# Hash products and sums of the late attention pairs grouped ahead of a half's scores, and weight stores on GpSimd's queue: one change to an attention and SwiGLU kernel

## Chip, cores and metric

The kernel runs on one core of a Trainium2 chip. The metric is the device time of one execution in microseconds (us), the median of several. The engines are TensorE (PE: matmuls; PEld are its weight loads), VectorE (DVE), ScalarE (ACT), GpSimd (POOL) and SyncE (SP); POOL, SP and ACT can issue DMA transfers, each from a queue of its own that is worked in order.

## What is computed

Attention in which a query sees only the keys of its own hash bucket (the signs of six projections), over 4 batches and 8 heads of 768 positions by 64, and behind it a SwiGLU block on the 3072 x 512 result.

```python
q_bits = (einsum('bhsd,dk->bhsk', q, proj) > 0)          # 6 bits, same for k
mask = q_bucket[:, :, :, None] == k_bucket[:, :, None, :]
scores = where(mask, scale * (q @ k.T), -1e9)
attn = exp(scores - max) / (sum + 1e-9)
x = (attn @ v).transpose(0, 2, 1, 3).reshape(3072, 512)
g = x @ w_gate;  val = x @ w_val
out = (g * sigmoid(g) * val) @ w_out                     # d_ff 1536
```

The three weight matrices arrive as 8-byte floats, of which the kernel makes single-precision parts itself.

## The kernel before

**Attention.** Two heads make a pair; 16 pairs are worked one after the other (n from 0 to 15), each in two halves of 384 query rows (half 0 and 1). A half has six key chunks of 128. For each chunk `score` (L436 to L450) runs the score products and on top of them the hash products of q and k signs (`qb`, `kb`), so that keys of another bucket drop out, and ACT writes the exponentials into one of eight buffers `A`. DVE adds the exponentials up in `acc` (`add`, L478 and L482). Behind the six chunks, `attend` (L460) multiplies them by v, and ACT copies the result to `xT` (L471).

The score, hash, sum and transpose products take their PSUM tiles from one pool, "ps", of 7 banks in rotation: an eighth tile waits until the first one's last reader is through.

For each pair there is work besides:

- the operands of the next pair (`front`). For late pairs (n + 1 > 4) two DVE transposes (L413) come behind half 0's scores, and then one group of eight hash products (L372) whose tile ACT reads in four sign operations (L377). `hash_next` does the two q signs at once, sends them to a second place by a DMA on SP (L389), and returns the two k signs and DVE's mask products (L386) as a list `rest` for later. Before, the group stands behind chunk 2 of half 1, and `rest` is worked behind all six chunks.
- the sums of the pair before (`total`, L487 to L499): four products of `acc` with ones (L493), a copy on ACT (`row`, L496), a DMA to `few` (L498). Then `invert` (L502 to L511): a reciprocal on DVE, a DMA to DRAM (`sums`) and two back (`r`); then `norm` (L517) multiplies on DVE and stores `xT` (L522). Before, the sums stand behind chunk 1 of half 0, `invert` behind half 0's scores, and `norm` behind half 1's.
- loads of the pair after next on SP: q and k (L271, eight DMAs behind chunk 2 of half 1, in runs of 128 bytes for late pairs) and v (L250).
- four or five steps of the weight preparation (`prepare`), which fill idle time of DVE and ACT.

**Weight preparation.** 36 pieces. For each one, POOL loads `words` (L120), ACT scales them (`scale`, L127 and L128) into a `stage` buffer (three of them), DVE does three steps (L153, L155, L158), ACT rounds (`round_up`, L135), DVE does two more (L167, L169), and a DMA stores the buffer to DRAM (`ram`, L171). `scale_ahead` (L137) scales the next piece i if i < kept + ahead, where kept is the number of pieces whose store has been issued; ahead is 3 in attention and is set to 2 ahead of the gated block. Scaling piece i overwrites the buffer of piece i-3, so it waits until that store has landed. 26 stores are issued by the end of attention, on POOL; for the other ten, and the last seven `words` loads, `queues[0]` is SP.

**The gated block.** Per batch 12 blocks of hidden columns: for each one ("U"), a gate piece g and a value piece v, each with products "a" and "n" of 2.8 and 1.4 us on PE (L600), ACT's copy of a (L642), DVE's subtraction (L648), SiLU (L650), the product (L652) and the hidden parts (L653 to L658); after each three, the output products ("D", six chunks). Their PSUM tiles are four, of two banks each, in rotation ("pp"). Weight pieces come from DRAM through a ring of seven buffers (`bring`, L207, on POOL). Behind each of these atoms (four in a U, six in a D) the loop calls `prepare_on(1)` and then `scale_ahead()`, so one step of the weight preparation follows each atom.

The order on each engine is that of the program text, and waits between engines are set by the framework from the data.

Of the kernel before, what the change touches and what calls it, by code (L numbers as in the profile page):

```python
# [8 lines left out]
FP32 = mybir.dt.float32  # L9
# [10 lines left out]
def kernel(  # L20
# [20 lines left out]
    nc = tc.nc  # L41
# [8 lines left out]
    NP = H // 2  # L50
# [27 lines left out]
    def r32(t):  # L78
        return t.bitcast(FP32R)

    def finish(todo):
        while todo:
            todo.pop(0)()
# [12 lines left out]
    n = 0  # L96
# [8 lines left out]
    NPIECE = len(pieces)  # L105
    ram = [dram.tile([P, 3, PIECE], FP32R, tag=f"ram{i}", name="ram") for i in range(NPIECE)]
    words = {}
    staged = {}
    progress = {"scaled": 0, "kept": 0, "ahead": 3}

    queues = [nc.gpsimd]

    def load_words(count, queue=None):
        queue = queue or queues[0]
        for i in range(len(words), min(count, NPIECE)):
            words[i] = t = wordp.tile([P, PIECE, 2], I32, tag="words", name="words")
            to = t.rearrange("p f w -> p (f w)")
            if len(pieces[i].shape) == 3:
                to = to.rearrange("p (j c) -> p j c", j=NJ)
            queue.dma_start(to, pieces[i])  # L120

    def scale(i):
        t = words[i]
        staged[i] = st = stagep.tile([P, 3, PIECE], FP32, tag="stage", name="stage")
        top = t.rearrange("p f w -> p (f w)").bitcast(U16)
        top = top.rearrange("p (f w) -> p f w", w=4)[:, :, 1]
        nc.scalar.activation(st[:, 1], t[:, :, 1].bitcast(FP32), AF.Copy, scale=2.0**-112)  # L127
        nc.scalar.activation(t[:, :, 0], top, AF.Copy, scale=2.0**-13 * (1 + 2.0**-17))  # L128
        progress["scaled"] = i + 1
# [3 lines left out]
    def round_up():  # L133
        st = staged[unrounded.pop(0)]
        nc.scalar.activation(r32(st[:, 0]), st[:, 1], AF.Copy, scale=TOWARD)  # L135

    def scale_ahead():  # L137
        if unrounded:
            round_up()
        i = progress["scaled"]  # L140
        if i < NPIECE and i < progress["kept"] + progress["ahead"] and i in words:
            scale(i)

    def prepare():
        for i in range(NPIECE + 1):
            if i < NPIECE:
                load_words(i + 1)
                if i not in staged:
                    scale(i)
                t, st = words[i], staged[i]  # L150
                lo, hi = t[:, :, 0], t[:, :, 1]
                wi = st[:, 1].bitcast(I32)
                nc.vector.tensor_single_scalar(wi, wi, 3, op=ALU.logical_shift_left)  # L153
                yield True
                nc.vector.scalar_tensor_tensor(out=wi, in0=hi, scalar=-(1 << 31), in1=wi,  # L155
                                               op0=ALU.bitwise_and, op1=ALU.bitwise_or)
                yield True
                nc.vector.tensor_tensor(wi, wi, lo, op=ALU.add)  # L158
                unrounded.append(i)
                load_words(i + 3)  # L160
                yield True
            if i > 0:
                while i - 1 in unrounded:
                    round_up()
                st = staged[i - 1]
                w = st[:, 1]
                nc.vector.tensor_tensor(r32(w), w, st[:, 0], op=ALU.subtract)  # L167
                yield True
                nc.vector.scalar_tensor_tensor(out=r32(st[:, 2]), in0=w, scalar=-STEP,  # L169
                                               in1=st[:, 0], op0=ALU.mult, op1=ALU.add)  # L170
                queues[0].dma_start(ram[i - 1].bitcast(FP32), st)  # L171
                progress["kept"] = i
                yield True

    preparing = prepare()

    def prepare_on(n):
        for _ in range(n):
            next(preparing, None)
# [51 lines left out]
    def attention(scope):  # L231
# [44 lines left out]
        def load(n, names):  # L276
            if n < len(pairs):
                for name in names:
                    fetch(n, name, nc.sync)
# [151 lines left out]
        waiting = []  # L431
# [4 lines left out]
        def score(u):  # L436
            n, half, c = units[u]
            qs = slice(half * HQ, (half + 1) * HQ)
            ks = slice(c * P, (c + 1) * P)
            sc = [bank("sc")[:, 0:HQ] for _ in range(2)]  # L440
            for x, start in ((T, True), (bits, False)):
                if u < 2 and not start:
                    prepare_pair(1)
                for h in range(2):
                    rows = slice(h * D, (h + 1) * D)
                    nc.tensor.matmul(sc[h], x["k", n][rows, ks], x["q", n][rows, qs],  # L446
                                     start=start, stop=not start)
            for h in range(2):
                nc.scalar.activation(weights(u)[:, h, 0:HQ], sc[h], AF.Exp,  # L449
                                     scale=SCALE * (OFF / 2 if n <= NP else 1.0))  # L450
# [22 lines left out]
        def add(u):  # L473
            n, half, c = units[u]
            a = weights(u)
            if c == 1:
                acc[n, half] = att.tile([P, 2, HQ], FP32, tag="acc", name="acc", bufs=3)
                nc.vector.scalar_tensor_tensor(out=acc[n, half], in0=weights(u - 1)[:, :, 0:HQ],  # L478
                                               scalar=S * EPS / P, in1=a[:, :, 0:HQ],
                                               op0=ALU.add, op1=ALU.add)  # L480
            elif c > 1:
                nc.vector.tensor_tensor(acc[n, half], acc[n, half], a[:, :, 0:HQ], op=ALU.add)  # L482
# [4 lines left out]
        def total(n):  # L487
            ps = bank("sum")
            t = [acc.pop((n, half)) for half in range(2)]
            for h in range(2):  # L490
                for half in range(2):
                    g = (2 * h + half) * BLOCK
                    nc.tensor.matmul(ps[g : g + BLOCK, 0:HQ], ones, t[half][:, h, :],  # L493
                                     start=True, stop=True)
            row = att.tile([P, HQ], FP32, tag="row", name="row", bufs=1)
            nc.scalar.copy(row, ps[:, 0:HQ])  # L496
            few = small.tile([P, each], FP32, tag="few", name="few")
            nc.sync.dma_start(few, row.rearrange("(g r) t -> r g t", r=BLOCK)[0])  # L498
            waiting.append(lambda: invert(n, few))  # L499
# [27 lines left out]
        rest = []  # L527

        def prepare_pair(count):
            for _ in range(count):  # L530
                if steps:
                    rest.extend(f for f in steps.pop(0)() or [] if f)
# [4 lines left out]
        last = []  # L537
        for u in range(0, N, NCH):
            n, half, _ = units[u]
            more = n + 1 < len(pairs)  # L540
            for c in range(NCH):
                score(u + c)
                if u + c == 2 or more and half == 1 and c == 2:
                    prepare_pair(1)
                if half == 1 and c == 2:
                    load(n + 2, "qk")
                if c == 1 and half == 0 and n > 0:
                    total(n - 1)
                if c:
                    add(u + c)  # L550
            finish(rest)
            if half == 0 and more:
                steps = front(n + 1)
                if u:
                    prepare_pair(2)
            if half == 0:
                while waiting:
                    last.append(waiting.pop(0)())
            else:
                finish(last)  # L560
            for _ in range(1 if u else 2):
                scale_ahead()
            for c in range(NCH):
                attend(u + c)
            scale_ahead()
            if half == 1:
                load(n + 2, "v")
            elif more:
                if n + 1 <= NP:
                    prepare_pair(2 if u else 4)  # L570
            prepare_on(5 if 0 < n < NP else 4)
            if u >= N - 7 * NCH:
                bring()
# [5 lines left out]
    with ExitStack() as scope:  # L579
        attention(scope)  # L580
# [3 lines left out]
    def gated_block(scope):  # L584
        rest = scope.enter_context(tc.tile_pool(name="odd_x_rest", bufs=1))
# [118 lines left out]
                        end(c)  # L704
                    yield chunk

        queues[0] = nc.sync
        progress["ahead"] = 2
        tails = []
        splits = []  # L710
        count = [0]
# [27 lines left out]
    with ExitStack() as scope:  # L739
        gated_block(scope)  # L740
# [32 lines left out]
```

## Time and profile before

| | |
|---|---|
| median of 3 runs | 961.79 us (961.63 to 964.93) |
| the profiled execution's own time | 961.79 us |
| its span | 960.0 us |
| attention, about | 0 to 358.6 us |
| gated block, about | 358.6 us to the end |
| one late pair where nothing waits | 20.12 us (hash group to hash group, 259.42 to 279.54) |
| a `ring` load, 768 KB | 5.6 us from issue to landing (median) |
| a `ram` store on POOL, 768 KB | 4.7 us (median of 26) |

The span runs from the first to the last instruction. In a row of the timeline, the first two numbers are start and length in us; then come engine, line, operation and operands, how many instructions were merged, and in brackets the idle time ahead of the row and what ended it. A line number is one of the kernel before; the changed kernel's numbers differ by up to 7.

### The profile page before, as it was taken

The numbers are of one execution on the slowest core, as the hardware profiler recorded it, in microseconds if no ns is written. First come the engines' busy times: TensorE is split into PE (matmuls) and PEld (weight loads), VectorE is DVE, ScalarE is ACT, GpSimd is POOL, SyncE is SP. The second block draws the span as 40 slices with busy tenths as digits, with TensorE's granted clock in tenths as the row PEclk, the third lists the DMA queues.
The fourth block names the chain that finished last, engine by engine and source line by source line (L and its number), as shares of the span: only waits on it lengthen the run. The fifth ranks groups of instructions, "written<-read, shape, count | busy, mean of one in ns | idle before, by whom it ended". The sixth has DMA issues, their size and how long they took to land.

```text
span 960.0 us, 14459 instructions
## 1 busy us (share of the span) xinstructions
PE 938.3 (98%) x5413; PEld 715.0 (74%) x5413; DVE 672.0 (70%) x868; ACT 473.7 (49%) x882; POOL 114.7 (12%) x231
## 2 busy tenths in 40 slices
PE   8999989999999799999999999999999999999997
PEld 4444434444444349999999999999999999999996
DVE  4788878888888586878766545766546686446556
ACT  6899777777877565443331332421332422332311
POOL 3110011100101011111111011011111111110100
PEclk9999999999999899999999999999999999999999
DMA  6567567886888868896676565565754655754641
GB/s 187 161 179 205 141 168 200 193 214 173 228 191 251 204 227 295 304 386 262 255 263 250 194 232 191 186 218 207 282 197 141 238 204 184 270 196 134 237 158 67
DMA packets 135798, 203.22 MB, mean 212 GB/s; under 512 B 92912, under 2 KB 100560, under 8 KB 135728
## 3 DMA queue, kind: packets, MB, share of 16 engines
q0 software_dynamic: 28560, 148.26, 43.5%
q1 hardware_dynamic: 106368, 53.84, 21.4%
q8 instruction: 43, 0.70, 0.3%
q10 hardware_dynamic: 800, 0.20, 0.1%
q14 instruction: 27, 0.22, 0.1%
HBM read 162.01 MB, written 39.42 MB: 210 GB/s over the span
## 4 chain that ended last, share of the span: by engine, by line
PE 89%; DMA 4%; ACT 2%; SPq 2%; DVE 2%; issue 1%; ACTq 0%; DVEq 0%; POOLq 0%
PE a L600 28%; PE o L600 20%; PE sc L446 14%; PE n L600 14%; PE av L460 10%; DMA qb<-qb 3%; SPq L271 2%; ACT A L449 1%; PE sum L493 1%; PE hps L372 1%; PE tps L359 1%; DMA xram<-xT 1%; ACT qb L377 1%; DVE o L692 0%; DVE o L689 0%
## 5 line engine op out<-in xcount | busy, mean ns | idle before, releaser
L600 PE MATMUL a<-xparts,ring 128*128 128x384 f32 x1536 | 282.2, 334 | 0.6 <-ACT row L496 0.6
L600 PEld LDWEIGHTS a<-xparts,ring 128*128 128x128 f32 x1536 | 268.1, 188 | 2.5 <-ACT row L496 1.3
L600 PE MATMUL o<-ring,hid 128*128 128x512 f32 x864 | 199.1, 390 | 0.0
L600 PEld LDWEIGHTS o<-ring,hid 128*128 128x128 f32 x864 | 161.9, 188 | 33.1
L449 ACT ACTIVATE A<-sc 128x384 f32<-128x384 f32 x384 | 157.7, 508 | 21.7 <-PE sc L446 21.2
L446 PE MATMUL sc<-qT,kT 64*128 64x384 f32 x768 | 165.6, 505 | 0.2 <-ACT A L449 0.2
L600 PE MATMUL n<-xparts,ring 128*128 128x384 f32 x768 | 148.5, 334 | 0.0
L482 DVE TENSOR_TENSOR acc<-acc,A 128x768 f32<-128x768 f32 x128 | 122.7, 958 | 23.5 <-ACT A L449 12.2
L207 POOL DMA_DIRECT2D ring<-ram x144 | 75.9, 529 | 494.8 <-PE n L600 321.6
L600 PEld LDWEIGHTS n<-xparts,ring 128*128 128x128 f32 x768 | 134.5, 188 | 0.0
L460 PE MATMUL av<-A,vraw 128*64 128x386 f32 (+1 forms) x768 | 131.2, 490 | 0.0
L648 DVE TENSOR_TENSOR v<-v,n 128x768 f32<-128x768 f32 x48 | 45.8, 954 | 111.4 <-PE n L600 109.6
L446 PEld LDWEIGHTS sc<-qT,kT 64*128 64x128 f32 x768 | 69.4, 189 | 70.9 <-issue 53.0
L460 PEld LDWEIGHTS av<-A,vraw 128*64 128x64 f32 x768 | 52.3, 136 | 71.9 <-issue 59.1
L642 ACT ACTIVATE g<-a 128x768 f32<-128x768 f32 x48 | 39.0, 812 | 126.3 <-PE a L600 126.3
L653 ACT ACTIVATE hid<-v 128x768 fp32r<-128x768 f32 x48 | 40.7, 848 | 119.9 <-DVE v L652 119.9
L650 ACT ACTIVATE g<-g 128x768 f32<-128x768 f32 x48 | 40.6, 846 | 87.6 <-DVE g L648 87.6
L692 DVE TENSOR_TENSOR o<-o 128x512 f32<-128x512 f32 x96 | 66.0, 687 | 21.5 <-ACT o L687 19.0
L446 PE MATMUL sc<-qb,kb 64*128 64x384 bf16 x384 | 68.8, 325 | 6.2 <-DMA qb<-qb 4.4
L648 DVE TENSOR_TENSOR g<-g,n 128x768 f32<-128x768 f32 x48 | 45.6, 950 | 34.2 <-PE n L600 31.0
L656 DVE SCALAR_TENSOR_TENSOR hid<-hid,v 128x768 fp32r<-128x768 f32 x48 | 45.9, 957 | 26.9 <-ACT hid L653 26.9
L689 DVE SCALAR_TENSOR_TENSOR o<-o 128x512 f32<-128x512 f32 x72 | 49.5, 687 | 12.0 <-PE o L600 11.4
(77 smaller groups left out, 671.1 us busy)
## 6 DMA issues: line engine op xcount, KB each, us to landing
ring<-ram POOLq DMA_DIRECT2D x144, 768.0 KB, 5.6
ram<-stage POOLq DMA_DIRECT2D x26, 768.0 KB, 4.7
ram<-stage SPq DMA_DIRECT2D x10, 768.0 KB
vraw<-in_v_dram SPq DMA_DIRECT2D x16, 384.0 KB
out_dram<-o SPq DMA_DIRECT2D x24, 256.0 KB
r<-sums SPq DMA_DIRECT2D x30, 192.0 KB
qraw<-in_q_dram SPq DMA_DIRECT2D x48, 96.0 KB
words<-in_moe_w_gate_dram POOLq DMA_DIRECT2D x9, 512.0 KB, 7.0
```

The lines of the kernel that those rows point to most:

```text
L207: nc.gpsimd.dma_start(t.bitcast(FP32), ram[at].bitcast(FP32))
L446: nc.tensor.matmul(sc[h], x["k", n][rows, ks], x["q", n][rows, qs], start=start, stop=not start)
L449: nc.scalar.activation(weights(u)[:, h, 0:HQ], sc[h], AF.Exp, scale=SCALE * (OFF / 2 if n <= NP else 1.0))
L460: nc.tensor.matmul(ps[h * D : (h + 1) * D, 0:width], raws["v", n][:, h, c, :], a[:, h, 0:width], start=c == 0, stop=c == NCH - 1)
L482: nc.vector.tensor_tensor(acc[n, half], acc[n, half], a[:, :, 0:HQ], op=ALU.add)
L600: nc.tensor.matmul(ps, w, x, start=start, stop=stop)
L648: nc.vector.tensor_tensor(two(z), two(z), n_, op=ALU.subtract)
L650: nc.scalar.activation(z, z, AF.Silu)
L653: nc.scalar.activation(h, val, AF.Copy, scale=TOWARD / STEP)
L656: nc.vector.scalar_tensor_tensor(out=l, in0=h.bitcast(FP32), scalar=-STEP, in1=val, op0=ALU.mult, op1=ALU.add)
L689: nc.vector.scalar_tensor_tensor(out=accs[c], in0=t[:, 0], scalar=STEP + 1, in1=accs[c], op0=ALU.mult, op1=ALU.add)
L692: nc.vector.tensor_tensor(accs[c], accs[c], t[:, 1], op=ALU.subtract)
```

## The change

In attention:

- `total(n - 1)` moves from behind chunk 1 of half 0 to ahead of half 1's scores (pairs 1 to 14; the last pair keeps its place).
- For late pairs the hash group moves from behind chunk 2 of half 1 to ahead of half 1's scores, right behind the sums. Its k signs and DVE's mask products follow behind chunk 1 of that half instead of behind its last chunk.
- `invert` moves behind half 1's scores, and `norm` behind the next pair's half 0.

In the weight preparation, the switch of queue and of `ahead` is gone: stores and words stay on POOL, and `ahead` stays 3 in the gated block.

```diff
-    progress = {"scaled": 0, "kept": 0, "ahead": 3}
-    queues = [nc.gpsimd]
-    def load_words(count, queue=None):
-        queue = queue or queues[0]
+    progress = {"scaled": 0, "kept": 0}
+    def load_words(count, queue=nc.gpsimd):
...
-        if i < NPIECE and i < progress["kept"] + progress["ahead"] and i in words:
+        if i < NPIECE and i < progress["kept"] + 3 and i in words:
             scale(i)
...
-                queues[0].dma_start(ram[i - 1].bitcast(FP32), st)
+                nc.gpsimd.dma_start(ram[i - 1].bitcast(FP32), st)
...
             more = n + 1 < len(pairs)
+            final = not more
+            late = n + 1 > NP
+            if half == 1 and n > 0 and not final:
+                total(n - 1)
+            if half == 1 and more and late:
+                prepare_pair(1)
             for c in range(NCH):
                 score(u + c)
-                if u + c == 2 or more and half == 1 and c == 2:
+                if u + c == 2 or more and half == 1 and c == 2 and not late:
                     prepare_pair(1)
+                if half == 1 and c == 1 and late:
+                    finish(rest)
                 if half == 1 and c == 2:
                     load(n + 2, "qk")
-                if c == 1 and half == 0 and n > 0:
+                if c == 1 and half == 0 and final:
                     total(n - 1)
...
+            if half == 1:
+                finish(last)
+            while waiting and (half == 1 or final):
+                last.append(waiting.pop(0)())
             if half == 0:
-                while waiting:
-                    last.append(waiting.pop(0)())
-            else:
-                finish(last)
+                finish(last[:-1] if final else last)
+                last[:] = last[-1:] if final else []
...
-        queues[0] = nc.sync
-        progress["ahead"] = 2
```

## The prediction

> **What bounds it now.** I read the page's busy shares and chain first, then busy time by stage, then the order of events on each engine around the moved instructions. The chain of what ended last is TensorE (PE) nearly everywhere:
>
> ```profile
> PE 938.3 (98%) x5413; PEld 715.0 (74%) x5413; DVE 672.0 (70%) x868; ACT 473.7 (49%) x882; POOL 114.7 (12%) x231
> ...
> PE 89%; DMA 4%; ACT 2%; SPq 2%; DVE 2%; issue 1%; ACTq 0%; DVEq 0%; POOLq 0%
> ```
>
> So each term below is a change of PE's time: an instruction group that gets shorter, or a gap. By stage (columns: window, its length, then busy us of PE, PEld, DVE, ACT, POOL, clock, DMA share, GB/s):
>
> ```profile
> 110.00:358.60 248.60, 234.46 (x1550) 102.23 (x1546) 205.48 (x277) 184.62 (x419) 24.95 (x42) 0.98 0.76 201
> 358.60:470.00 111.40, 111.40 (x604) 106.48 (x605) 86.12 (x118) 50.63 (x73) 14.76 (x28) 1.00 0.85 318
> ```
>
> In the late pairs PE has 14.1 us of gaps. In the gated block's first 111 us, where the last weight pieces are made, it has none. Whatever the change adds there is paid in full.
>
> **Part 1, the grouped products.** One hash group between scores, in PE's order of time (start, length):
>
> ```profile
> 258.51 0.81 PE L446 MATMUL sc<-qT,kT 64*128 64x384 f32 x4
> 259.16 0.33 PE L446 MATMUL sc<-qb,kb 64*128 64x384 bf16 x2
> 259.42 0.52 PE L372 MATMUL hps<-qT,hash 128*32 128x384 f32 x2
> ...
> 260.20 0.92 PE L446 MATMUL sc<-qT,kT 64*128 64x384 f32 x4
> 260.95 0.33 PE L446 MATMUL sc<-qb,kb 64*128 64x384 bf16 x2
> 261.11 0.81 PE L446 MATMUL sc<-qT,kT 64*128 64x384 f32 x4
> ```
>
> Chunks of scores follow each other every 0.81 us. The chunk before the group lasts 0.91, the group 0.78, the chunk after it 0.91: an inserted group costs 0.98. The sum group costs the same (267.76 to 270.36 is 2.60 for two chunks and a group). Set between value products and scores, where PE changes its shape anyway (4.02 us from value products to sum at the end of attention, 4.03 to scores elsewhere), a group costs 0.78. A late pair loses two insertions: 20.12 - 0.40 = 19.7 us if nothing waits. Three early pairs move only the sum: -0.2 each, -0.6 together.
>
> **Part 2, a new wait for a PSUM bank.** The pool "ps" has 7 banks in rotation. In the new order a second half takes: sum 1, hash 2, chunk 0: 3 and 4, chunk 1: 5 and 6, chunk 2: 7 and then 1 again (the sum's), chunk 3: 2, the hash's. That bank is free only after all four sign operations, and the two k signs now stand behind chunk 1's exponentials on ScalarE (ACT). From the hash group's start h: q signs start at h+0.92 (131.77 to 132.69 in one pair where ACT had waited for them), two take 1.18, four exponentials 1.62, two k signs 1.2; ends at h+4.9. PE wants the bank at h + 0.78 + 0.91 + 0.81 + 0.81 = h+3.3. Wait 1.6 us, each late pair. Before, the hash's bank came round only in the next half.
>
> ```profile
> 260.34 1.16 ACT L377 ACTIVATE qb<-hps,columns 32x384 bf16<-32x384 f32 x2
> 261.52 2.41 ACT L449 ACTIVATE A<-sc 128x384 f32<-128x384 f32 x6
> 263.95 1.18 ACT L377 ACTIVATE kb<-hps,columns 32x384 bf16<-32x384 f32 x2
> ```
>
> Period 19.7 + 1.6 = 21.3 against 20.12: +1.2 x 11 = **+13.3**. VectorE (DVE) comes to the same length: from h+4.9 the mask products 0.85, five adds 5.2, reciprocal and four weight steps 2.6, the next half's adds (their first exponentials arrive at h+14.3) 5.2, two transposes 1.85, then the next hash group at h+21.4. So it adds nothing yet, but its slack is gone. Ends for this part: 0 if the bank is free in time, and 22 (the wait and 0.8 of DVE more in each pair).
>
> What goes: the late copy of the q signs (`qb`) and its kin. SP now issues it before the next loads, and not behind the sums' and r's round trip, and PE reaches the hash 2.4 us earlier.
>
> ```profile
> 143.68 0.32 PE L446 MATMUL sc<-qb,kb 64*128 64x384 bf16 x1 [3.04 <-DMA qb<-qb]
> ...
> 144.76 1.50 PE L493 MATMUL sum<-acc,ones 128*32 128x384 f32 x8
> ...
> 328.98 0.86 PE L372 MATMUL hps<-qT,hash 128*32 128x384 f32 x2 [7.20 <-DVE qT L413]
> ```
>
> The first costs 0.2 + 3.04, and the slow 3.2 us behind it (1.7 elsewhere) 1.5 more; smaller waits of 0.47, 0.42, 0.58, 0.37 and 1.07 go too: **-7.7**. The 7.2 us is a wait for pair 15's loads (kraw, 8.8 us of DVE idle). They start 3.3 us earlier, but the hash is wanted 2.4 earlier too, in a pair that is 1.2 longer: about **-1.5**. Moved on SP: few, qb, eight loads, then sums, r, vraw, xram. xram no longer stands ahead of vraw; r now issues some 5 us before its norm instead of 7 to 9. Its late landing falls into 1.5 us of DVE idle before the mask products; without that cover it joins the DVE end above. Attention in sum: -0.6 + 13.3 - 7.7 - 1.5 = **+3.5** (-14 without the bank wait, +12 at the DVE end).
>
> **Part 3, the gated block.** Two things return: stores and words on POOL, and scaling three pieces ahead of the last store instead of two. The stage pool has three buffers, so scaling piece i needs the store of piece i-3 landed. With two ahead that store was issued a piece earlier; with three, `scale_ahead` comes right after the step that issues it. Before, ACT passed such a place without waiting:
>
> ```profile
> 369.28 0.85 ACT L653 ACTIVATE hid<-v 128x768 fp32r<-128x768 f32 x1 [2.62 <-DVE v L652]
> 370.03 0.65 ACT L127 ACTIVATE stage<-words 128x512 f32<-128x512 f32 x1
> 370.59 0.66 ACT L128 ACTIVATE words<-words 128x512 int32<-128x512 uint16 x1
> 371.15 0.79 ACT L642 ACTIVATE g<-a 128x768 f32<-128x768 f32 x1
> ```
>
> The store's landing is shown in attention, where three ahead already holds:
>
> ```profile
> 309.29 0.67 ACT L127 ACTIVATE stage<-words 128x512 f32<-128x512 f32 x1 [2.71 <-DMA ram<-stage]
> ```
>
> The step L169 had ended at 303.26, so 6.0 us; three more such give 5.3, 6.3 and 7.1. All 26 POOL stores land 3.6/4.7/6.5 us (least, median, most) after issue; with 0.6 from the step to the issue, 4.2 to 7.1. I take 5.5. Ring loads ahead of it on POOL have 7.2 us here against 5.6 overall, a reason not to go lower.
>
> The first two of eight: piece 28's scale waits for store 25 (issued 359.58, landed about 364.3): ACT is 1.2 late, and with scaling's 1.2 moved up, v's copy ends at 369 instead of 366.7. DVE's step for piece 26 ends at 371.6, its store lands at 377.1. ACT has finished hid at 371.7 and stands 5.3 us; behind it wait scaling (1.2) and g's copy (0.8), done at 379.1. That copy frees the accumulator that PE wants at 375.35 (PE's row "375.35 2.93 PE L600" of g2): a gap of 3.7. Carried down the compiled order in the same way, with four two-bank tiles in rotation, the gaps are 3.7, 3.8, 0.6 + 5.6, 2.3 + 5.1, 3.8, 4.6, 1.0: **+30**. Six landings are on that chain, so the sum is 6 x landing - 2.7: 22 at 4.2 us, 40 at 7.1. Below nothing it can't be: PE has no gap there to give back. After the last store PE runs as before.
>
> The POOL queue itself I cost at nothing: the 17 loads and stores take 0.5 to 0.8 us each, the ring load ahead of a store waits for the same PE products as DVE's step, and ring loads run seven pieces ahead (some 29 us cover; a POOL delay beyond that would reach PE one to one).
>
> The Trainium skill speaks against giving the queue any weight: DMA: Bandwidth & Descriptors, section Issuing engines are not separate DMA queues, says that DMAs of all issuers share 16 engines and a second issuer saves only issue time. This trace's issues, 0.32 us on SP and 0.54 on POOL, fit; were the queue all that differs, part 3 would be 0. It isn't: the order of ACT changes.
>
> After 3.04 us of gap PE was slow (above), after 1.07 it wasn't. Six gaps here exceed 3.04; at 1.5 each they would add up to 9, but ACT sets the pace, so I take 0. The Trainium skill, TensorE: Matmul & The Clock Gate, section HAM oscillation — how this bites in real kernels, has the clock halve after gaps of some 3.4 us; the 3.04 here lies under that, so the measurement decides, and by either the six gaps are long enough.
>
> **Sum.** The profiled execution is 961.79 us (span 960.0 and 1.8 around it), which is also the median. 961.8 + 3.5 + 30 = **995**.
>
> **Rivals.**
> - No bank wait (hash bank free before chunk 3, because signs run sooner or banks go round otherwise): attention -14, gated +30: 978. For it: ACT is only 74% busy in these pairs. Against: the count of banks.
> - Faster: stores land before ACT needs them. The place is the scale behind hid; g's copy has 375.35 - 371.94 = 3.4 us of cover, so from landings of 3.4 us down the gaps go, and with attention at -14 it gives 948. Against: no store landed under 3.6 + 0.6. If the bank wait holds as well it is 965, no change.
> - Worse: DVE's lost slack shows in each pair (+12 in all), landings at 7.1 (40) and slow PE after gaps (9): 1022.
> - That the grouped order isn't what the program does: excluded, the compiled PE order has sum, hash, scores in 11 pairs.
>
> **Numbers.** Forecast 0.64 (984 to 1010); no bank wait 0.16; worse 0.10; faster 0.06; within 0.5% 0.04. Range 972 to 1014, which leaves out some of the worse case and the faster ones. By 0.5%, about what a measurement of this kernel can tell from no change: faster 0.06, same 0.04, slower 0.90.
>
> **What would show it.** Right: ACT idle of about 5 us on stage L124 <- DMA ram<-stage seven times after attention; PE gaps on L607 of 4 to 6 us there; a PE gap of 1.6 us at chunk 3 of each late second half, behind kb's signs; late period 21.3; no qb wait. Wrong: a late period near 19.7 (no bank wait), PE without gaps after attention (landing hidden), or PE waiting for qT in each pair (DVE).

## The result, and the profile after

The changed kernel takes **1020.37 us** (median of 4 runs, 1017.17 to 1024.35) beside 963.36 for the kernel before (961.63 to 965.81): ratio 1.059, 95% interval 1.054 to 1.064. Slower, as forecast, but by 57 us and not by 33; it lies above the range. The profiled execution took 1021.44 us, its span is 1019.5.

Line numbers of the changed kernel are 3 lower than before in attention and 7 higher in the gated block (hash L369, scores L443, `mean` L467, norm L514, `scale` L124, gated products L607). On its page, PE's busy time and the chain:

```profile
PE 968.9 (95%) x5413; PEld 737.9 (72%) x5413; DVE 672.5 (66%) x868; ACT 470.4 (46%) x882; POOL 124.9 (12%) x248
...
PE 50%; issue 5%; DMA 3%; DVE 2%; ACT 1%; ACTq 0%; POOLq 0%
PE a L607 22%; PE o L607 16%; PE n L607 11%; DMA ram<-stage 3%; DVE o L699 1%; DVE o L696 0%; ACT words L125 0%; ACT stage L124 0%; DVE v L655 0%; DVE hid L663 0%; ACT g L657 0%; ACT v L649 0%; DVE v L659 0%; DVE stage L152 0%; ACT L657 0%
```

Two things to see. `DMA ram<-stage`, a store, is now a link of the chain. And the same 5413 matmuls are "busy" for 968.9 us instead of 938.3: half of the 59.5 us of longer span is recorded as work, so a list of PE's gaps can't show it.

The first gated product starts at 389.58 us; before it was 358.60. So attention is 31.0 us longer and the gated block 28.5 (629.9 to the end, 601.4 before). Busy time by stage, the late pairs first (columns as in the prediction):

```profile
112.00:389.58 277.58, 256.63 (x1565) 120.22 (x1565) 208.39 (x281) 186.28 (x428) 24.95 (x42) 0.95 0.70 180
389.58:500.00 110.42, 89.93 (x440) 82.31 (x441) 62.05 (x86) 39.88 (x59) 18.60 (x33) 0.92 0.66 234
```

Late pairs: 20.9 us of gaps where there were 14.1, but 22 us more of busy time for about the same matmuls, at a clock of 0.95 instead of 0.98. Gated stage: 20.5 us of gaps where there were none, clock 0.92 instead of 1.00.

**A late second half.** ACT, DVE and PE of one pair, from its timeline:

```profile
227.61 0.70 ACT L125 ACTIVATE words<-words 128x512 int32<-128x512 uint16 x1
232.69 0.17 ACT L467 ACTIVATE e<-av 128x1 f32<-128x1 f32 x1 [4.38 <-DVE xT L514]
232.75 0.47 ACT L468 COPY xT<-av 128x384 f32<-128x384 f32 x1
233.11 0.50 ACT L493 COPY row<-sum 128x384 f32<-128x384 f32 x1
233.48 1.15 ACT L374 ACTIVATE qb<-hps,columns 32x384 bf16<-32x384 f32 x2
234.66 1.64 ACT L446 ACTIVATE A<-sc 128x384 f32<-128x384 f32 x4
236.32 1.16 ACT L374 ACTIVATE kb<-hps,columns 32x384 bf16<-32x384 f32 x2
```

```profile
228.89 0.93 DVE L410 STREAM_TRANSPOSE qT<-qraw 128x768 f32<-128x768 f32 x1
231.57 1.02 DVE L514 SCALAR_TENSOR_TENSOR xT<-xT,e,r 128x768 f32<-128x768 f32 x1 [1.75 <-DMA r<-sums]
...
237.52 0.85 DVE L383 TENSOR_SCALAR kb<-kb,columns 32x768 bf16<-32x768 bf16 x2 [2.54 <-ACT kb L374]
```

```profile
229.07 0.85 PE L490 MATMUL sum<-acc,ones 128*32 128x384 f32 x8
229.88 0.52 PE L369 MATMUL hps<-qT,hash 128*32 128x384 f32 x2
...
232.38 0.81 PE L443 MATMUL sc<-qT,kT 64*128 64x384 f32 x2
233.66 0.59 PE L443 MATMUL sc<-qT,kT 64*128 64x384 f32 x1 [0.48 <-ACT row L493]
...
235.20 1.35 PE L443 MATMUL sc<-qT,kT 64*128 64x384 f32 x3 [0.47 <-ACT A L446]
```

Read it from DVE. Its norm (L514) now stands behind the transposes, and r lands late: it ends at 232.59. ACT has been idle since 228.3. What it wants to do is tiny, the copy of one column of value products into `mean` (L467), 0.17 us; but `mean` has two buffers, so pair n's copy overwrites what the norm of pair n-2 still reads. Behind that copy on ACT stand the copy to xT, `row`, the q signs and the exponentials, all due some 4 us earlier. PE has run its groups and two chunks, and then goes at ACT's pace: short gaps, single matmuls in place of groups. From 235.7 to 239.0 the granted clock was besides 0.50, though no gap of PE ahead of it in this half was over 0.48 us. The k signs end at 237.48, and DVE stands 2.54 us for them with the adds queued behind.

The list of waits says how often (columns: engine, line, what it waited for, us in all, times, longest; from 100 to 390 us):

```profile
ACT e L467 <- DVE xT L514: 39.7, 7, 10.1
DVE kb L383 <- ACT kb L374: 26.5, 11, 2.7
DVE xT L514 <- DMA r<-sums: 14.3, 7, 3.0
...
ACT xparts L215 <- DVE xT L514: 11.0, 2, 6.3
PE sc L443 <- ACT row L493: 7.7, 7, 2.3
```

On PE itself only 7.7 us of it show, as waits for `row`.

**The gated block.** PE, then ACT, then the stores on POOL:

```profile
404.96 1.55 PE L607 MATMUL n<-xparts,ring 128*128 128x384 f32 x8
409.94 4.51 PE L607 MATMUL a<-xparts,ring 128*128 128x384 f32 x16 [3.42 <-ACT g L649]
...
415.68 2.93 PE L607 MATMUL a<-xparts,ring 128*128 128x384 f32 x16
...
425.60 3.05 PE L607 MATMUL a<-xparts,ring 128*128 128x384 f32 x16 [1.44 <-ACT v L649]
```

```profile
402.63 0.85 ACT L660 ACTIVATE hid<-v 128x768 fp32r<-128x768 f32 x1 [2.01 <-DVE v L659]
407.99 0.66 ACT L124 ACTIVATE stage<-words 128x512 f32<-128x512 f32 x1 [4.51 <-DMA ram<-stage]
408.55 0.64 ACT L125 ACTIVATE words<-words 128x512 int32<-128x512 uint16 x1
409.09 0.79 ACT L649 ACTIVATE g<-a 128x768 f32<-128x768 f32 x1
```

```profile
403.74 0.54 POOL L168 DMA_DIRECT2D ram<-stage  x1 [4.72 <-ACT hid L660]
...
418.43 0.78 POOL L168 DMA_DIRECT2D ram<-stage  x1 [11.09 <-issue]
```

This is the predicted chain: store issued at 403.74, ACT free to scale 4.25 us later, g's copy behind the scaling, PE behind g's copy. PE's gaps there are 3.42, 1.44, 5.86, 0.24, 5.49, 2.60, 0.42 and 1.03: 20.5 us. The first group after the gap of 3.42 took 4.51 us, the next like it 2.93.

### The profile page after: what moved, and what is told of

It reads as the page before. It is cut to its first block, busy times and chain, and to the rows that moved or that the text cites. A ratio compares the mean times of both kernels' runs of the same rounds, so it can differ in the third digit from the quotient of the medians.

```text
span 1019.5 us, 14489 instructions
## 1 busy us (share of the span) xinstructions
PE 968.9 (95%) x5413; PEld 737.9 (72%) x5413; DVE 672.5 (66%) x868; ACT 470.4 (46%) x882; POOL 124.9 (12%) x248
## 4 chain that ended last, share of the span: by engine, by line
PE 50%; issue 5%; DMA 3%; DVE 2%; ACT 1%; ACTq 0%; POOLq 0%
PE a L607 22%; PE o L607 16%; PE n L607 11%; DMA ram<-stage 3%; DVE o L699 1%; DVE o L696 0%; ACT words L125 0%; ACT stage L124 0%; DVE v L655 0%; DVE hid L663 0%; ACT g L657 0%; ACT v L649 0%; DVE v L659 0%; DVE stage L152 0%; ACT L657 0%
## 5 line engine op out<-in xcount | busy, mean ns | idle before, releaser
L607 PE MATMUL a<-xparts,ring 128*128 128x384 f32 x1536 | 285.0, 337 | 6.1 <-ACT g L649 3.4
L607 PEld LDWEIGHTS a<-xparts,ring 128*128 128x128 f32 x1536 | 270.8, 189 | 8.6 <-ACT g L649 3.7
L607 PE MATMUL o<-ring,hid 128*128 128x512 f32 x864 | 202.3, 393 | 10.1 <-ACT v L649 5.9
L443 PE MATMUL sc<-qT,kT 64*128 64x384 f32 x768 | 187.5, 527 | 14.1 <-ACT row L493 7.7
L607 PEld LDWEIGHTS o<-ring,hid 128*128 128x128 f32 x864 | 162.7, 189 | 45.8 <-ACT v L649 6.4
L446 ACT ACTIVATE A<-sc 128x384 f32<-128x384 f32 x384 | 155.1, 510 | 9.1 <-PE sc L443 8.5
L607 PE MATMUL n<-xparts,ring 128*128 128x384 f32 x768 | 149.9, 336 | 5.5 <-DVE o L699 5.5
L443 PEld LDWEIGHTS sc<-qT,kT 64*128 64x128 f32 x768 | 87.3, 198 | 84.2 <-issue 44.2
L607 PEld LDWEIGHTS n<-xparts,ring 128*128 128x128 f32 x768 | 135.5, 189 | 5.8 <-DVE o L699 5.8
L443 PE MATMUL sc<-qb,kb 64*128 64x384 bf16 x384 | 83.4, 336 | 0.6 <-DVE kb L383 0.5
L168 POOL DMA_DIRECT2D ram<-stage x36 | 19.7, 547 | 410.2 <-ACT A L446 175.6
```

What stands on the lines that cost most here:

```text
L607: nc.tensor.matmul(ps, w, x, start=start, stop=stop)
```

## The experiments

18 kernels. Times of "before" are those of the same set of runs; ratios are to these, with 95% intervals.

### Is it two independent costs? (a1, a3, a4, a5)

a1 is the changed kernel with the old lines of the weight preparation put back. a3, a4 and a5 are the kernel before with one or both of them changed:

```diff
a1, in the changed kernel:   +  queues[0] = nc.sync;  progress["ahead"] = 2
a3, in the kernel before:    -  queues[0] = nc.sync;  progress["ahead"] = 2
a4, in the kernel before:    -  progress["ahead"] = 2
a5, in the kernel before:    -  queues[0] = nc.sync
```

> The changed kernel with the gated block of before put back (stores and words on SP, two pieces ahead); attention as changed. If the two parts add up, the gated block has no PE gaps and takes 601 us again, attention stays at about 388: 992 us (988 to 997). Rival: the gated gaps are a consequence of attention ending with its weight pieces in another phase; then some gaps stay and the time lies above 1000.

> The kernel before with only the gated part changed: stores and words on POOL, three pieces ahead. If the parts add up: ACT waits of 4 to 8 us on the stores, PE gaps of some 20 us in sum and slow matmuls behind them, 990 us (986 to 996). Rival, that it needs the new attention: below 975 us.

> The kernel before with three pieces ahead in the gated block, but the queue left on SP. Theory that ACT's order (scaling right behind the store it needs) is all of it: 985 to 996 us, like three ahead on POOL. Rival, that POOL's queue (stores behind ring loads) is what makes the landing late: 965 to 978 us.

> The kernel before with stores and words of the gated block on POOL, two pieces ahead. If the order on ACT is all that costs, the queue costs nothing: 961 to 967 us. Rival, that POOL's queue delays the ring loads or the stores: 970 us or more.

Measured: a1 993.1 (1.029, 1.026 to 1.032); a3 991.4 (1.029, 1.026 to 1.032), both beside 964.7; a4 997.8 (1.035, 1.031 to 1.038); a5 964.6 beside 965.0 (0.9995, 0.997 to 1.002). The two parts alone cost 28.4 and 26.7 us, 55 of the 57 together. In the gated part everything is `ahead`; the queue alone, with two ahead, costs nothing. With three ahead SyncE's queue is 6 us worse than GpSimd's (a4 beside a3; a4 came out 2 us above what I had expected); why was not followed. ACT's waits for stores from 345 to 500 us, in a3:

```profile
ACT stage L127 <- DMA ram<-stage: 34.0, 6, 8.5
```

In a4 it is 43.2 us, 9 times; in a5 none is listed.

### Is it the buffer of `mean`? (a2, a6)

```diff
-                    mean[n] = small.tile([P, 1], FP32, tag="e", name="e")
+                    mean[n] = small.tile([P, 1], FP32, tag="e", name="e", bufs=4)
```

a2 is that in the changed kernel, a6 in a1.

> The changed kernel with four buffers instead of two for the small tile mean (tag e), nothing else. Theory M: ACT's copy into mean of pair n waits for norm of pair n-2, which now stands behind the transposes and the landing of r, and ACT's row copy, signs and exponentials wait behind it; with four buffers that wait is gone, late pairs go from 21 to 24 us to about 19.8 to 20.3, attention ends some 30 to 38 us earlier, total 983 to 992 us. Rival G: the grouping itself costs (signs ahead of exponentials on ACT, banks, DVE without slack); then the total stays above 1010 us, and late pairs take over 21 us.

> The changed attention with the old gated block and four buffers for mean. The two effects measured apart were 28 us (gated) and 12 to 16 us (mean): if they add up, 977 to 985 us. Rival, that the gated block hides part of attention's delay: above 988 us.

Measured: a2 1008.3 beside 964.7 (1.0455, 1.042 to 1.049), between the two theories; a6 982.8 beside 963.1 (1.019, 1.015 to 1.024). In a2 the wait of L467 for L514 is gone and attention is 16 us shorter in the profile (373.32 to the first gated product); by the ratios it brings 13 us in a2 and 9 in a6. So the missed wait is shown, but it is less than half of attention's loss. A late half of a2, PE:

```profile
202.45 0.52 PE L369 MATMUL hps<-qT,hash 128*32 128x384 f32 x2
...
204.95 0.81 PE L443 MATMUL sc<-qT,kT 64*128 64x384 f32 x4
205.60 0.33 PE L443 MATMUL sc<-qb,kb 64*128 64x384 bf16 x2
205.76 0.81 PE L443 MATMUL sc<-qT,kT 64*128 64x384 f32 x4
...
207.44 1.10 PE L443 MATMUL sc<-qT,kT 64*128 64x384 f32 x3
```

The hash's tile was still being read until the k signs' end, 207.39 on ACT, yet chunk 3 started at 205.76 without a wait, and chunk 5 at 207.44. The prediction had chunk 3 wait for the hash's bank; it does not. The first that can be waiting for it is chunk 5, and by under 0.1 us.

### What is the rest? One part at a time (a8, a9)

```diff
a8, before with the hash group alone moved:
+            if half == 1 and more and late:
+                prepare_pair(1)
...
+                if half == 1 and c == 1 and late:
+                    finish(rest)
a9, a1 without these lines: the hash behind chunk 2, the k signs at the end
```

> The kernel before with only the hash group moved ahead of half 1's scores, k signs and mask products behind chunk 1; sums, invert and norm stay. Theory M: norm is as early as before, so no wait for mean; the group costs 0.2 us less per pair, c5's bank wait about 0.5 more, waits for qb go (up to 7.7): 955 to 966 us. Rival G (the signs ahead of the exponentials and DVE's lost slack are what costs): 975 us or more.

> The changed kernel with the old gated block and the hash group back behind chunk 2, its k signs at the end: only sums, invert and norm are moved. Theory M: ACT waits for norm at mean and at the split as in the changed kernel, row and exponentials late, 978 to 993 us. Rival G: without the hash group ahead of the scores the loss is gone, 960 to 970 us.

Measured: a8 973.9 (1.010, 1.006 to 1.014), between the two theories; a9 988.3 (1.024, 1.021 to 1.028), as theory M had it. The sums, `invert` and norm alone cost 25 us, nearly all of attention's loss; ACT's waits in a9 from 100 to 390 us show the same wait as in the changed kernel:

```profile
ACT e L470 <- DVE xT L517: 54.8, 10, 10.9
```

The hash alone, which I had expected to be no slower than before, costs 10 us; the two costs don't add (36 us beside the 28 of a1). In a8 every one of 11 late hash groups waits for DVE's transposes (16.1 us in all, 6.6 of it in pair 15), and DVE waits for the k signs in every pair (28.4 us, 11 times): hash, signs, masks, adds, transposes and the next hash are one closed chain, 21.2 to 22.4 us around.

### Taking the waits away one after the other (a7, a10, a12, a11, a14)

a7 is a6 with the norm behind half 0's value products; a10 is a7 with the k signs behind the last chunk; a12 is a10 with the late pairs' transposes behind chunk 3 of half 0. a11 and a14 do the last two to a8, the hash alone.

```diff
a7    the block "if half == 0: finish(last...)" moves behind the loop over attend
a10, a11:
-                if half == 1 and c == 1 and late:
-                    finish(rest)
a12, a14:
+                if c == 3 and half == 0 and more and late:
+                    steps = front(n + 1)
+                    prepare_pair(2)
```

> As the run with four mean buffers and the old gated block, and norm with batch 0's split placed behind the value products of half 0 instead of ahead of them, so that neither mean nor the split's first operation on ACT (17.7 us of waiting for norm) stands ahead of the xT copy, the row copy and the signs. Theory M (what is left is ACT waiting for norm in another place): 965 to 975 us, and no PE gap behind row at 110 to 145 us. Rival G (the rest is the grouping's): no more than 3 us under the run without this edit, near 980.

> The run with norm behind the value products, and the k signs and mask products back behind half 1's last chunk. Theory D: with the hash group ahead of the scores, hash, signs, DVE's adds and the next transposes make a closed loop of 21 to 22 us; in it DVE stands still some 2 us for the k signs ahead of the mask products. With these at the end the loop is about 20.2 us, a pair takes 20.0 to 20.4: 966 to 974 us. Rival (the loss is in DMA, late r and q/k loads): no change, 978 to 982 us.

> As the run with signs last, and the two transposes of late pairs behind chunk 3 of half 0 instead of behind chunk 5, two adds (2.1 us) earlier. Theory D: the hash no longer waits for DVE and a pair takes PE's own 19.7 to 20.0 us: 958 to 968 us. Rival: the transposes then stand still for the q and k loads and hold up the adds: 970 us or more.

> The kernel before with only the hash group ahead of half 1's scores, and k signs and mask products at the end as before. Theory D: without the k signs' 2 us ahead of the adds the loop is about 20.3 us, the hash waits for transposes go down to 0.5 us or less per pair, waits for qb are gone: 958 to 966 us. Rival (that the q signs ahead of the exponentials cost by themselves): 970 to 975 us, as with the k signs early.

> Before with the hash group alone ahead of half 1's scores, k signs behind the last chunk (970.1 us), and the two transposes of late pairs behind chunk 3 of half 0 instead of behind its scores. Theory L (the hash waits about 0.42 us in each of ten pairs for the transposes, 9 us with what stands behind it, and the earlier transposes end before PE wants them): 961-967, ratio 0.996 to 1.002 of before. Rival (DVE's order is full either way; the adds of half 0 come 1.85 us later, hold the buffers of the exponentials, and the masks come late as in the variant with both groups): 968-975.

Measured: a7 980.2 (1.016, 1.011 to 1.020), a10 976.5 beside 965.0 (1.012, 1.007 to 1.017), a12 980.0 (1.014, 1.010 to 1.019), a11 970.1 (1.004, 1.002 to 1.007), a14 964.6 beside 963.6 (1.002, 1.000 to 1.004). a7, a10 and a12 lie above what I expected of them by 5 us, 3 and 12, a11 by 4. From a6 on, each of these steps lies within the interval of the one ahead of it; only a6 to a10 together, 1.019 to 1.012, stands out of the noise, and barely. In a12 PE's wait for the masks grew from 9.8 us in a10 to 14.7. a14 came out as theory L had it: freed of nearly all of both waits, the hash alone is level with the kernel before, not faster.

How long each pair takes (us; from the end of the value products of one pair's second half to the next, read off the timelines):

```
pair      3    4    5    6    7    8    9   10   11   12   13   14   15    end
before 22.0 20.4 21.6 25.4 20.8 20.1 21.0 20.1 20.1 20.1 20.8 30.2 19.1  357.2
after  26.1 26.5 24.2 22.8 21.2 24.0 23.9 21.2 24.4 21.2 25.0 30.9 20.9  387.6
a2     26.2 26.4 24.1 20.4 20.4 20.4 20.6 20.7 20.4 21.7 20.4 33.2 19.1  369.2
a10    24.8 25.2 22.2 20.5 21.1 19.7 26.1 19.7 19.7 20.9 19.7 33.5 19.1  367.5
a14    22.0 20.5 21.6 25.1 19.9 19.9 21.5 19.9 19.9 20.5 21.7 32.5 19.1  359.4
```

This table settles what the sums could not. In a10 the undisturbed late pair takes 19.7 us, 0.4 less than before, just what part 1 of the prediction gives. What is lost is lost in a few pairs: 3 and 4 (7.6 us), 9 (5.1) and 14 (3.3); pair 6 gains 4.9. Pair 9 of a10, on SyncE, DVE and then PE:

```profile
182.16 6.86 SPq L271 DMA_DIRECT2D qraw<-in_q_dram  x4
...
191.93 1.58 SPq L504 DMA_DIRECT2D sums<-few  x1
198.16 1.12 SPq L511 DMA_DIRECT2D r<-sums  x2
```

```profile
203.70 1.02 DVE L517 SCALAR_TENSOR_TENSOR xT<-xT,e,r 128x768 f32<-128x768 f32 x1 [4.96 <-DMA r<-sums]
...
207.95 4.15 DVE L482 TENSOR_TENSOR acc<-acc,A 128x768 f32<-128x768 f32 x4
212.13 0.85 DVE L386 TENSOR_SCALAR kb<-kb,columns 32x768 bf16<-32x768 bf16 x2
```

```profile
208.64 0.92 PE L446 MATMUL sc<-qT,kT 64*128 64x384 f32 x4
213.13 0.50 PE L446 MATMUL sc<-qb,kb 64*128 64x384 bf16 x2 [3.58 <-DVE few L502]
213.40 1.51 PE L446 MATMUL sc<-qT,kT 64*128 64x384 f32 x4
```

r is 5 us late (`sums` goes out behind the loads' issues, 6.86 us for q alone, and r another 6.2 us later), the norm with it, then the adds, then the masks, and PE stands 3.58 us for the masks (the releaser named is DVE's next, short step, right behind them). Behind that gap three chunks take 1.5 us of score products in place of 0.8, at a granted clock of 0.50 (212.0 to 218.6). In pairs 3 and 4 norm's wait for r (2.7 and 2.4 us in a10) reaches PE over ACT, whose step of `split` (L218) needs the norm.

### Can r's round trip be taken out of the way? (a13, a15, a16, a17, a18)

In the changed order SyncE issues `sums` and r behind eight q/k loads. a13 is a10 with `invert` ahead of the loads, a15 the same with a12's transposes. In both, norm came forward along with invert, into the same half 1, which I had not meant; a16 and a17 are the same two with norm kept behind the next half 0. a18 is a10 with sums and r issued by GpSimd.

```diff
a16, a17 (a13, a15 append to last at once):
                 if half == 1 and c == 2:
+                    new = [f() for f in waiting]
+                    waiting.clear()
                     load(n + 2, "qk")
...
             if half == 1:
                 finish(last)
+                last.extend(new)
a18, in invert, but for the last pair:
-            nc.sync.dma_start(s, few)
+            nc.gpsimd.dma_start(s, few)
...
-                nc.sync.dma_start(t[...], flat[...])
+                nc.gpsimd.dma_start(t[...], flat[...])
```

> The kernel 'norm and signs last' (grouped sums and hash, mean with four buffers, norm behind the attends, k signs last, old gated block; 976.5 us beside 965.0) with invert emitted ahead of the q/k loads in half 1, so that SyncE issues sums and r before the eight loads and not behind them. Theory R (what is left is r's late landing: DVE stands about 20 us at norm, and masks and adds behind it are late): that wait falls under 5 us, PE's wait for the masks goes, 963-970 us, ratio 0.998 to 1.006. Theory L (DVE's closed chain of hash, signs, adds and transposes sets the pace whatever r does): 972-979, r's wait gone but DVE idle elsewhere by as much. A third outcome: SyncE now stands 2 to 3 us for the sums' store before the loads, the loads land later and the transposes wait for kraw: 975-985.

> Both: 'norm and signs last' with invert ahead of the q/k loads and the transposes behind chunk 3 of half 0. Theory R+L (each removes its own wait): 955-965, at or below before, which would make the grouped order as good as the old one once nothing in it waits. Rival (DVE's chain remains): 970-982.

> The variant with invert ahead of the q/k loads, mended: there the norm came forward by a stage along with invert, into the same half 1, ahead of its value products, and DVE still stood for r (26 us, 11 times). Here invert is ahead of the loads and norm stays where 'norm and signs last' (976.5 beside 965.0) has it, behind the next pair's half 0 attends. Theory R (r's late landing is what is left): DVE's wait for r falls under 5 us and the time to 963-971. Theory L (DVE's closed chain of transposes, hash, signs, masks sets the pace): r's wait goes, the time stays at 972-980 and PE waits for qT at the hash groups instead. Third: loads 3 us later, DVE waits for kraw: 980 and over.

> The same with the late pairs' transposes behind chunk 3 of half 0. Theory R+L (each removes its own wait): 957-966, at about the time before. Rival (the late second halves' DVE work does not fit between transposes and masks): 970-982. With the hash alone the earlier transposes gave 964.6 beside 963.6, so theory L predicts that they help here too, by 4 to 6 us against the run above.

> 'Norm and signs last' (976.5 beside 965.0; DVE stands 20.1 us for r, 9 times, and PE 9.8 us for the masks behind it) with the stores of sums and the two loads r of pairs 0 to 14 issued by GpSimd's queue, whose own loads and stores there are four to five per pair, and not by SyncE's behind eight q/k loads. The q/k loads keep their place, so the cost that invert ahead of them had (kraw 43.2 us, 9 times) should not come. Theory Q (the place in SyncE's queue makes r late): DVE's wait for r falls under 6 us, 964-971, ratio 0.999 to 1.007. Rival T (r is late because its data, and that of sums, land slowly while the q/k loads' small runs are on the DMA engines, whoever issues them): r wait stays at 15-25 us, 973-980. Third: r wait goes and the time stays at 973-980, so that the masks and adds wait for something else.

Measured: a13 998.0 (1.035, 1.033 to 1.038), a15 995.0 (1.032, 1.030 to 1.035), a16 1008.5 beside 963.9 (1.047, 1.043 to 1.050), a17 1026.5 (1.065, 1.061 to 1.068), a18 980.6 beside 964.0 (1.018, 1.016 to 1.020). a13 and a15 don't test the theory: DVE still stood 26.4 and 33.8 us for r (11 times each, from 100 to 365 us). a16 took that wait away in full, and the loads paid for it. Waits of PE and of DVE from 100 to 390 us in a16:

```profile
PE hps L372 <- DVE qT L413: 45.9, 10, 10.8
```

```profile
DVE kT L413 <- DMA kraw<-in_k_dram: 43.2, 9, 10.8
```

and SyncE in one late half of a16:

```profile
224.01 0.32 SPq L504 DMA_DIRECT2D sums<-few  x1
226.81 1.13 SPq L511 DMA_DIRECT2D r<-sums  x2
227.99 2.76 SPq L271 DMA_DIRECT2D qraw<-in_q_dram  x4
230.79 3.48 SPq L271 DMA_DIRECT2D kraw<-in_k_dram  x4
```

In a10 the loads go out right behind the q signs' DMA (at most 0.4 us); in these rows of a16 they go out 7.1 us behind it (it had ended at 220.87). Of that SyncE stood 3.1 us for DVE's reciprocal, and 2.8 for sums, since r can't be issued until sums has landed; in that time nothing else goes out on this queue. kraw was then ready only at 240.98. SyncE's own waits, from 100 to 390 us, put the two side by side:

```profile
SPq L511 <- DMA sums<-few: 39.5, 12, 5.8
SPq L504 <- DVE few L502: 33.1, 12, 3.7
```

In a17 the earlier transposes only wait longer for kraw (73.0 us, 11 times, beside 43.2 and 9). In a18 r's wait is nearly gone too (1.6 us), and it is ACT that waits, for the weight stores queued behind that round trip on GpSimd (in three places from 196 to 244 us one goes out 2.5 to 3.2 us after DVE's last step on it, where a10 has 0.6). ACT's waits for stores from 100 to 372 us, which in a10 are 15.3 us, 7 times:

```profile
ACT stage L127 <- DMA ram<-stage: 30.1, 8, 8.5
```

So r's round trip blocks whichever of the two queues it is put on, and in the new order something urgent is behind it on both. Expected was theory Q, 964 to 971; it fell, and what I had named as the third outcome came: r in time and nothing gained. A version in which the trip is in nobody's way was not found, and no version beats the kernel before.

## Why the prediction was wrong, point by point

- **Attention, +3.5 (ends -14 and +12): measured +28.4 (a1).** This is the term that failed; its 25 us are the whole of what the forecast lacked. Its working asked of each moved instruction when its data come, and of PSUM when a bank is free; it never asked who waits for a buffer that norm still reads. Norm was moved by half a pair, and `mean` has two buffers. Moving the sums and norm alone costs 25 us (a9); giving `mean` four buffers brings 9 to 13 us (a6, a2). The 20 us that a6 still lacks are traced by rows to the chain of the next point and to norm's wait for r.
- **"VectorE comes to the same length ... so it adds nothing yet, but its slack is gone": wrong.** The chain I counted (next hash at h+21.4) is closed, so its length is the pace by itself: in a8 the late pairs take 21.2 to 22.4, through DVE. Moving the k signs to the end and the transposes forward takes this off again (a8 to a14, 1.010 to 1.002); by the medians the k signs make some 5 us of it (a11, 1.004) and the transposes 2 to 3, with intervals that overlap.
- **The PSUM bank wait of 1.6 us, +13.3: not there.** I let the seven banks go round strictly. a2's chunk 3 starts 1.6 us before the k signs are through. That rests on rows; in which order banks are handed out instead I only argue (it fits that a freed bank is taken first: chunk 2's second tile in the pair shown waits for `row`, which frees the sum's). The period of 21.3 that I forecast for it was near the hash-alone variant's, for another reason.
- **Early pairs, -0.6: wrong.** Pairs 3 and 4 lose 10.2 us after the change, and still 7.6 in a10. Moving the sum moves the norm there as well (a9, the sums alone, has the same 10.2), and ACT's `split` waits for it.
- **Part 1, 0.4 saved in each late pair: right**, 20.1 to 19.7 in a10, and too small to matter here. The moved hash alone gives 0.2 of it (a14).
- **The waits for qb, -7.7: they went** (no wait of that kind is listed for after), and attention grew all the same. **The kraw stall at pair 15, -1.5: stayed**, 7.3 us after and 7.2 before.
- **Gated block, +30: right in size, +28.5 in the profile and 26.7 alone (a3); in part by luck.** ACT waited for a store seven times after attention, 36.3 us in all, as forecast. My landing of 5.5 us counted from the end of DVE's step to ACT's scaling; in the six waits that end from 407.99 to 483.91 it was 4.2 to 6.4 us, 30.6 in sum, and by my own formula that makes 30.6 - 2.7 = 27.9 us of gaps. There were 20.5. The other 8.0 us of the 28.5 are PE's busy time (604.5 us from the first gated product to the end, 596.5 before), most of it slower matmuls after the long gaps: 1.6 after 3.42, 1.6 after 5.86, 2.5 after 5.49. I had this term at 0 because ACT sets the pace. Whether the slow matmuls fill time in which PE would have stood, or come on top of gaps that I put too high, no run tells. The queue at nothing: right with two ahead (a5); with three, GpSimd's was 6 us better than SyncE's (a3 beside a4).
- **The rivals.** "Worse" had 1022, within 2 us of what came, from DVE's slack, late landings and slow PE. DVE's chain and slow PE are in the runs; the landings were a little under what I took, not late, and the wait on `mean` was not in it at all. "No bank wait", 978, had its condition met, and the time was 42 us higher: a rival whose condition holds is still worth nothing if another wait was missed.

Settled are the two halves of the loss, `ahead`, `mean`, and the places of the k signs and the transposes together. The last 11.5 us (a10) are a net sum: by rows, pairs 3, 4 and 9, in which norm waits for r, lose 12.7 and pair 14 3.3, and pair 6 gains 4.9 (in pairs 3 and 4 ACT also waits 1.5 and 2.3 us for a store). That these losses would go with r in time is not shown, since each way of bringing it earlier blocked something else. Pair 14's 3 us were not followed.

## What to carry to other kernels

Where a step is moved, list not only what it needs but what it still holds: the buffer that its last read frees, however small, and the in-order engine that wants to overwrite it; a one-column copy of 0.17 us stood in front of ACT's whole queue. Compare the stage's busy time for the same instructions before and after, not only its gaps: here half of the loss was recorded as PE working, in part at half the clock. And a store or a round trip through DRAM needs a place in a queue where nothing urgent follows; scaling one buffer further ahead than the stores allow turned landings of 4 to 6 us into 27 us of loss.

## What the runs showed of the hardware

- In the gated block of the changed kernel PE's first groups after gaps of 3.42, 5.49 and 5.86 us were slow (4.51 us instead of 2.93 for 16 matmuls after the first; granted clock 0.51 from 409.8 to 413.2), after 1.44 and 2.60 us they were not (3.05 and, for nine output products, 2.34, as elsewhere). The Trainium skill, TensorE: Matmul & The Clock Gate, section HAM oscillation — how this bites in real kernels, puts the limit at about 3.4 us, and these five agree with it. Other rows don't: PE was slow after 3.04 us in the kernel before and after 1.96 us in a4 (4.61 us for 16 matmuls; clock 0.51 from 398.7 to 402.0), and the late half shown above had a clock of 0.50 behind gaps of 0.48 us at most. After 3.16 us in a12 PE was not slow (0.82 us a chunk; clock 1.00 from 212.3 to 216.0). So the length of the one gap ahead does not settle it.
- Stores of 768 KB landed 3.5 to 11.5 us after issue in the changed kernel, median 4.3; in the attention of before the median was 4.7.
- Four loads in runs of 128 bytes occupied SyncE for 2.76 us, but at times for 6.86 (q in a10, the rows of pair 9 above), and what stands behind them on that queue went out as much later.
